# Attention in 64-token halves with their own decay reference, and TensorE's order written out: one change to a fused attention and expert kernel

## The chip, the core and the metric

The kernel runs on one core of a Trainium2 chip. The core has five engines that run side by side, each with its own queue of instructions, and they wait for one another by semaphores. TensorE multiplies matrices into PSUM. VectorE (DVE in the profile) and ScalarE (ACT) work on SBUF and PSUM. GpSimd (POOL) works on SBUF. SyncE (SP) only issues transfers here, and ScalarE and GpSimd issue some too. The metric is the device time of one execution in microseconds (us). A time is the median of several executions; the profile comes from one execution of its own.

## What is computed

Two parts, one after the other. The attention is a gated linear recurrence over 768 tokens, for 4 batches of 8 heads with 48 columns each. The experts are a balanced assignment of 3072 tokens to 8 experts of 384 tokens each, and a two-layer network per expert.

```
f = 1 / (1 + exp(-f_logit))
for t in range(S):
    state = f[t][:, None] * state + outer(k[t], v[t])     # 48 x 48 per head
    y[t] = q[t] @ state
x = y with the heads side by side                         # 3072 x 384
logits = x @ w_gate                                       # 3072 x 8
order = argsort(-logits.flatten())                        # tokens go to experts, best first,
                                                          # 384 tokens at most for each
out[tokens of e] = relu(x[tokens of e] @ w1[e]) @ w2[e]
```

## The kernel before

**Attention.** The recurrence is worked in chunks of 128 tokens, 24 of them (6 of one batch, c = 0 to 5, for 4 batches, and the four batches take turns). With g = -log f, the sum L of g from a reference token to token t turns the decay into factors: q is multiplied by exp(-L) and k by exp(L). In before the reference lies in the middle of the chunk of 128. Inside a chunk, the products of all q and k (`scores`, tile A) are masked to the lower triangle with a predicated copy (tile am) and multiplied by v (`outputs`, tile Y). What came from earlier chunks sits in a state of 48 by 48 for each head. It is moved to the chunk's reference by a factor gl (tile R, made by GpSimd) and multiplied by q into the same Y. The state is R plus the chunk's own sum of k times v (`states`, tile dS).

**Stages and steps.** `attention(first, last)` is a software pipeline. In step s, stage n works on chunk s - n. The stages of before are `decays` (f to g), `gates` (L, the factors eq and ek, the sums "ends" over each half of the chunk, gl, and qg and kg), `states` (the transposes T of qg and kg, R and dS), `scores`, `outputs`, `transposed` (x transposed for the next stage, tile X) and `gate` (the router's logits, and x with its logits written to DRAM as xd). Loads of f, q, k and v are issued by SP two chunks ahead in the program, and run as far ahead as buffers allow: five for f, q and k, eight for v. The order of the instructions on each engine is set by a scheduler, except where `tc.manual_schedule` names an engine: there it stays as the program has it. Each engine then takes its instructions strictly in that order.

**PSUM.** PSUM has eight banks. Six rotate among the tiles L, T, A, dS and X, and two hold Y. A tile that takes a bank waits until the readers of the tile six places earlier are done.

**Shapes.** A matmul's stationary operand fills 128 rows and up to 128 columns of the array, or a part: the profile writes 128*64 where it has 64 columns and 48*64 where it has 48 rows. Matmuls on different parts of the array run at the same time. The profile shows two records for each float32 matmul, and one for a transpose.

**Routing and experts.** After the attention come the router's search (a chain of small DVE and TensorE instructions) and the experts' networks (lines 495 and 506). The latter are written in a fixed order in which pieces of network are placed between the search's instructions. GpSimd gathers rows of xd for each expert (`fetch`, tile xe) and the logits of 768 leftover tokens (tile lg). `load_weights` loads 3.1 MB for each expert in two transfers. The first two experts' weights have memory of their own (pool `early`), the next three take the attention's memory when it is free. In before, expert 0's weights load during the attention. Of expert 1, w1 waits until the rows of expert 0 have been fetched (`behind`: ScalarE copies one fetched number into the tile, and the transfer has to follow that copy). Its w2 and the next experts' weights have no such wait.

Of the kernel before, what the change touches and what calls it, by code (L numbers as in the profile page):

```python
# [10 lines left out]
FP32 = mybir.dt.float32  # L11
# [13 lines left out]
def kernel(  # L25
# [49 lines left out]
    spans = const([128, NT, 2, HP], FP32, "spans")  # L75
# [6 lines left out]
    def kept(shape, dtype, name):  # L82
# [5 lines left out]
    mask = kept([128, 128], I32, "mask")  # L88
    nc.vector.tensor_copy(out=mask[:], in_=wcum[:])
    nc.vector.tensor_scalar(out=wcum[0:64, :], in0=wcum[0:64, :],  # L90
                            scalar1=-1.0, scalar2=None, op0=ALU.add)


    ind = kept([128, 2], FP32, "ind")
    nc.vector.memset(ind[:], 0.0)
    nc.vector.memset(ind[0:64, 0:1], 1.0)
    nc.vector.memset(ind[64:128, 1:2], 1.0)
# [6 lines left out]
    a_bufs = [kept([128, 2, HP, 128], FP32, f"am{i}") for i in range(NB)]  # L104
# [29 lines left out]
    def gates(G):  # L134
        i = G["i"] % NB
        g = g_bufs[i]
        L = ps("L")
        Lv = L[:, 0:D].rearrange("t (h d) -> t h d", d=DH)
        nc.tensor.matmul(out=Lv, lhsT=wcum[:], rhs=g[:, :, 0:DH], start=True, stop=True)  # L139
        ends = L[:, D:D + 2 * HP].rearrange("p (n a) -> p n a", a=HP)  # L140
        for hp in range(HP):
            for r in range(2):
                nc.tensor.matmul(out=ends[DP * r:DP * r + DP, :, hp], lhsT=g[:, 2 * hp + r, :],  # L143
                                 rhs=ind[:], start=True, stop=True)
        eq = work.tile([128, H, DH], FP32, name="eq", tag="eq")
        ek = work.tile([128, H, DH], FP32, name="ek", tag="ek")
        dl = work.tile([128, H, DH], FP32, name="dl", tag="dl")
        nc.vector.tensor_scalar(out=dl[:], in0=Lv, scalar1=LIMIT, scalar2=-LIMIT,  # L148
                                op0=ALU.min, op1=ALU.max)
        nc.scalar.activation(out=eq[:], in_=dl[:], func=AF.Exp, bias=0.0, scale=-1.0)  # L150
        nc.scalar.activation(out=ek[:], in_=dl[:], func=AF.Exp, bias=0.0, scale=1.0)  # L151
        span = spans[:, G["i"]]
        nc.vector.tensor_copy(out=span, in_=ends)

        if G["c"]:
            gl = work.tile([128, HP], FP32, name="gl", tag="gl", bufs=3)
            nc.gpsimd.tensor_tensor(out=gl[:], in0=span[:, 0], in1=spans[:, G["i"] - B, 1],  # L157
                                    op=ALU.add)
            nc.scalar.activation(out=gl[:], in_=gl[:], func=AF.Exp, bias=0.0, scale=-1.0)
            G["gl"] = gl  # L160
        qg, kg = q_bufs[i], k_bufs[i]
        nc.vector.tensor_tensor(out=qg[:, :, 0:DH], in0=G["q"][:], in1=eq[:], op=ALU.mult)  # L162
        nc.gpsimd.tensor_tensor(out=kg[:, :, 0:DH], in0=G["k"][:], in1=ek[:], op=ALU.mult)  # L163
        G.update(qg=qg, kg=kg)

    def states(G):
        b, c, v_ = G["b"], G["c"], G["v"]
        for nm, t, copy in (("qT", G["qg"], nc.scalar.copy), ("kT", G["kg"], nc.vector.tensor_copy)):
# [8 lines left out]

        R = None
        if c:
            R = work.tile([128, HP, DH], FP32, name="R", tag="R", bufs=5)  # L180
            nc.gpsimd.tensor_tensor(
                out=R[:], in0=state[b][:],
                in1=G["gl"][:].unsqueeze(2).to_broadcast((128, HP, DH)), op=ALU.mult)
        G["R"] = R
        if c == NCH - 1:
            return
        dS = ps("dS")
        for hp in range(HP):
            for r in range(2):
# [1188 lines left out]
```

## Time and profile before

| | us |
|---|---|
| median of 9 runs | 488.05 |
| lowest and highest run | 486.75 and 496.04 |
| the profiled execution's own time | 489.63 |
| its span, from first to last instruction | 487.8 |
| attention: last logits copied at | 170.7 |
| TensorE busy between 30 and 140 | 108.5 of 110 |
| TensorE busy between 168 and 190 (search) | 13.0 of 22 |
| TensorE busy between 222 and 488 (experts) | 254.1 of 266 |
| transfers' busy share between 30 and 140 | 0.89 |

A line of a group view names the source line, the engine, the operation, the tiles (out<-in), the shapes and the count. In a timeline, the first two numbers are the start and the length from the first start to the last end of the records that are merged in the line. In brackets is how long the engine had been idle and what ended that. "PEld" are weight loads of TensorE. A wait's line ends with its total, how many there were and the longest. Times of start are counted from the span's start.

### The profile page before, as it was taken

What the parts mean: (1) busy time and instruction counts of PE and PEld (TensorE: products, weight loads), DVE (VectorE), ACT (ScalarE), POOL (GpSimd) and SP (SyncE); (2) the same over time, 40 slices, a digit from 0 to 9 for tenths busy, and PEclk for the clock granted to TensorE, in tenths of its full rate; (3) what the DMA queues carried; (4) which work ended last, traced back from release to release, by engine and by line L of the source; (5) the groups of instructions that cost most, each with busy time, mean ns of one, the idle gap of its engine ahead of it and who ended that gap; (6) DMA issues with size and microseconds to landing.
All of it is one profiled execution on the core that took longest, in us unless ns stands there. A gap on an engine that the chain in (4) does not pass through costs nothing.

```text
span 487.8 us, 11676 instructions
## 1 busy us (share of the span) xinstructions
PE 454.0 (93%) x4996; PEld 322.4 (66%) x4996; DVE 157.6 (32%) x507; ACT 138.4 (28%) x366; POOL 105.5 (22%) x157
## 2 busy tenths in 40 slices
PE   2999999999999948999999999899999999999991
PEld 1678887887788735756566665768887656556550
DVE  7366556556566765023333332400000000000000
ACT  3355555545344200212121211213332221212200
POOL 3123343433133104710000100320003301301010
PEclk9999999999999959999999999999999999999997
DMA  9986989889941178970000000225993200200000
GB/s 153 187 165 147 187 178 189 187 187 260 251 159 38 69 262 307 265 272 17 6 28 1 32 1 16 55 63 176 315 321 93 71 0 34 66 16 34 0 34 20
DMA packets 118542, 59.28 MB, mean 122 GB/s; under 512 B 101841, under 2 KB 113105, under 8 KB 118481
## 3 DMA queue, kind: packets, MB, share of 16 engines
q1 hardware_dynamic: 111760, 44.06, 36.4%
q0 software_dynamic: 3264, 9.56, 6.5%
q10 hardware_dynamic: 3456, 4.82, 2.8%
q8 instruction: 41, 0.67, 0.6%
q14 instruction: 21, 0.16, 0.1%
HBM read 48.89 MB, written 9.54 MB: 120 GB/s over the span
## 4 chain that ended last, share of the span: by engine, by line
PE 71%; issue 16%; DVE 5%; POOL 5%; DMA 2%; ACT 0%; POOLq 0%; DVEq 0%
PE O L506 20%; PE H L495 19%; PE Y L225 5%; PE T L171 4%; PE L L139 4%; PE A L208 4%; PE L L143 3%; PE Y L235 2%; PE dS L190 2%; PE X L249 2%; PE cnt L564 2%; DMA lg<-xd,at_l 2%; PE X L260 2%; PE Xe L484 1%; POOL out_dram L512 1%
## 5 line engine op out<-in xcount | busy, mean ns | idle before, releaser
L495 PE MATMUL H<-xeT,w 128*128 128x256 f32 (+2 forms) x624 | 135.2, 369 | 1.9 <-DVE beyond L783 1.4
L506 PE MATMUL O<-w,hT 128*128 128x384 f32 x384 | 136.6, 494 | 0.0
L495 PEld LDWEIGHTS H<-xeT,w 128*128 128x128 f32 x624 | 97.7, 191 | 28.8 <-issue 1.6
L506 PEld LDWEIGHTS O<-w,hT 128*128 128x128 f32 x384 | 68.8, 190 | 37.0 <-issue 0.4
L512 POOL DMA_INDIRECT out_dram<-o,tok x24 | 23.5, 980 | 222.5 <-ACT o L511 218.3
L499 ACT ACTIVATE hT<-H 128x256 f32<-128x256 f32 (+2 forms) x104 | 38.3, 368 | 98.1 <-PE H L495 96.8
L213 DVE COPY_PREDICATED am<-mask,A 128x512 f32<-128x512 int32 x48 | 32.5, 730 | 31.1 <-PE A L208 31.1
L511 ACT COPY o<-O 128x384 f32<-128x384 f32 x24 | 11.5, 479 | 80.5 <-PE O L506 73.9
L545 POOL DMA_INDIRECT xe<-xd,tok x24 | 23.2, 966 | 42.3 <-DVE numb L299 28.9
L163 POOL TENSOR_TENSOR kg<-k,ek 128x384 f32<-128x384 f32 x24 | 25.5, 1062 | 27.8 <-ACT ek L151 22.0
L139 PE MATMUL L<-g,wcum 128*128 128x384 f32 x48 | 23.8, 580 | 7.4 <-DVE linef L333 7.4
L208 PE MATMUL A<-qT,kT 48*64 48x128 f32 x768 | 27.1, 278 | 0.8 <-issue 0.8
L225 PE MATMUL Y<-v,am 128*64 128x48 f32 x768 | 27.5, 224 | 0.0
L225 PEld LDWEIGHTS Y<-v,am 128*64 128x64 f32 x768 | 24.4, 138 | 3.9 <-issue 3.7
L487 ACT COPY xeT<-Xe 128x384 f32<-128x384 f32 x24 | 11.5, 478 | 43.4 <-PE Xe L484 43.4
L143 PEld LDWEIGHTS L<-ind,g 128*64 128x64 f32 x384 | 14.0, 145 | 14.7 <-issue 14.7
L208 PEld LDWEIGHTS A<-qT,kT 48*64 48x64 f32 x768 | 21.7, 137 | 1.3 <-issue 1.0
L564 PEld LDWEIGHTS <-above 128*31 128x31 f16 x264 | 8.8, 97 | 19.5 <-issue 10.5
L150 ACT ACTIVATE eq<-dl 128x384 f32<-128x384 f32 x24 | 12.6, 523 | 29.0 <-DVE dl L148 28.4
L148 DVE TENSOR_SCALAR dl<-L 128x384 f32<-128x384 f32 x24 | 13.4, 558 | 21.6 <-PE L L143 21.6
L171 PE MATMUL T<-ident,qg 128*128 128x128 f32 x96 | 16.6, 299 | 1.8 <-DVE qg L162 1.8
L157 POOL TENSOR_TENSOR gl<-spans 128x4 f32<-128x4 f32 x20 | 4.0, 201 | 64.4 <-DVE logits L265 44.7
(179 smaller groups left out, 459.7 us busy)
## 6 DMA issues: line engine op xcount, KB each, us to landing
w<-in_moe_w_dram SPq DMA_DIRECT2D x16, 1536.0 KB, 8.4
xd<-x ACTq DMA_DIRECT2D x24, 196.0 KB, 3.4
f<-in_f_logit_dram SPq DMA_DIRECT2D x24, 192.0 KB, 4.6
q<-in_q_dram SPq DMA_DIRECT2D x24, 192.0 KB, 4.7
k<-in_k_dram SPq DMA_DIRECT2D x24, 192.0 KB, 4.8
v<-in_v_dram SPq DMA_DIRECT2D x24, 192.0 KB, 4.6
xe<-xd,tok POOLq DMA_INDIRECT x24, 3.8
out_dram<-o,tok POOLq DMA_INDIRECT x24, 2.6
```

Of the source, the lines that this page charges most:

```text
L139: nc.tensor.matmul(out=Lv, lhsT=wcum[:], rhs=g[:, :, 0:DH], start=True, stop=True)
L143: nc.tensor.matmul(out=ends[DP * r:DP * r + DP, :, hp], lhsT=g[:, 2 * hp + r, :], rhs=ind[:], start=True, stop=True)
L163: nc.gpsimd.tensor_tensor(out=kg[:, :, 0:DH], in0=G["k"][:], in1=ek[:], op=ALU.mult)
L171: nc.tensor.transpose(out=T[:, 128 * hp:128 * hp + 128], in_=t[:, 2 * hp:2 * hp + 2, :].rearrange("t h d -> t (h d)"), identity=ident[:])
L208: nc.tensor.matmul(out=A[par][HC * j:HC * j + HC, 128 * hp:128 * hp + 128], lhsT=G["kT"][rows, hp, HC * j:HC * j + HC], rhs=G["qT"][rows, ...
L213: nc.vector.copy_predicated(am[:, par], mask[:].unsqueeze(1).to_broadcast((128, HP, 128)), A[par][:].rearrange("s (a t) -> s a t", t=128))
L225: nc.tensor.matmul(out=Y[par][HC * j:HC * j + HC, DH * hp:DH * hp + DH], lhsT=G["am"][:, par, hp, HC * j:HC * j + HC], rhs=G["v"][:, 2 * h ...
L495: nc.tensor.matmul(out=L["H"][:, 0:w], lhsT=slots[e][0][:, d, 128 * ft:128 * ft + 128], rhs=xT[:, d, 0:w], start=(d == 0), stop=(d == DC - 1))
L499: nc.scalar.activation(out=hT[:, ft, 0:w], in_=L["H"][:, 0:w], func=AF.Relu)
L506: nc.tensor.matmul(out=L["O"][:, 0:D], lhsT=hT[:, ft, 128 * i:128 * i + 128], rhs=slots[e][1][:, ft, :], start=(ft == 0), stop=(ft == FC - 1))
L512: nc.gpsimd.indirect_dma_start(out=outs[next(tiles)][:, :], out_offset=bass.IndirectOffsetOnAxis(ap=token(e, first_block + i), axis=0), in ...
L545: nc.gpsimd.indirect_dma_start(out=t[:], out_offset=None, in_=xd[:, :], in_offset=bass.IndirectOffsetOnAxis(ap=token(e, i), axis=0))
```

## The change

- **Halves.** The 128 tokens of a chunk become two halves of 64, each with a reference of its own in its middle. Matrix `wcum` becomes two blocks, the mask is 64 wide, and the sums over the chunk are taken for its four quarters. `scores` multiplies each half with itself alone: 64 columns instead of 128. What the second half owes to the first goes by the state: each chunk now has two R and two dS (except the last chunk of a batch, with one dS), and two updates of the state. Chunks with c = 0 get an R for their second half.
- **Y.** The products of am and v have 64 rows instead of 128. They are laid out so that upper and lower rows of the array write different banks. Some parts of a chunk's output then lie in two places. ScalarE copies one of them to SBUF (tile cross), and DVE adds them into x.
- **No clipping copy.** ScalarE's exponentials read L from PSUM. DVE's copy with limits (tile dl) is gone.
- **TensorE's order.** The attention's TensorE instructions stay as the program has them: L, transposes and X (128*128), then A, Y and dS (64 rows by 64 columns), then ends and the logits (128*64). Stages are split for that: `gates` into `cumulated` and `lengths`, `states` into `turned` and `states`. Ends and logits share a bank of their own (`step_bank`).
- **Small moves.** The logits go into x by GpSimd instead of ScalarE. Expert 1's weights load with expert 0's during the attention. The weights of experts 2, 3 and 4 now wait, w1 and w2 alike, for the fetched rows.

```diff
-    def gates(G):
+    def cumulated(G):
         i = G["i"] % NB
         L = ps("L")
...
-        nc.vector.tensor_scalar(out=dl[:], in0=Lv, scalar1=LIMIT, scalar2=-LIMIT,
-                                op0=ALU.min, op1=ALU.max)
-        nc.scalar.activation(out=eq[:], in_=dl[:], func=AF.Exp, bias=0.0, scale=-1.0)
-        nc.scalar.activation(out=ek[:], in_=dl[:], func=AF.Exp, bias=0.0, scale=1.0)
+        nc.scalar.activation(out=ek[:], in_=Lv, func=AF.Exp, bias=0.0, scale=1.0)
+        nc.scalar.activation(out=eq[:], in_=Lv, func=AF.Exp, bias=0.0, scale=-1.0)
+        qg, kg = q_bufs[i], k_bufs[i]
+        nc.gpsimd.tensor_tensor(out=kg[:, :, 0:DH], in0=G["k"][:], in1=ek[:], op=ALU.mult)
+        nc.vector.tensor_tensor(out=qg[:, :, 0:DH], in0=G["q"][:], in1=eq[:], op=ALU.mult)
...
+    def lengths(G):
+        r = step_bank()
+        ends = r[:, 0:4 * HP].rearrange("p (n a) -> p n a", a=HP)
...
+        nc.vector.tensor_copy(out=span, in_=ends)
+        gl = work.tile([128, 2, HP], FP32, name="gl", tag="gl", bufs=3)
+        nc.gpsimd.tensor_tensor(out=gl[:, 1], in0=span[:, 1], in1=span[:, 2], op=ALU.add)
+        first = 0 if G["c"] else 1
         if G["c"]:
+            nc.gpsimd.tensor_tensor(out=gl[:, 0], in0=span[:, 0], in1=spans[:, G["i"] - B, 3],
                                     op=ALU.add)
+        nc.scalar.activation(out=gl[:, first:2], in_=gl[:, first:2], func=AF.Exp, bias=0.0,
+                             scale=-1.0)
...
+    def states(G):
+        last = 1 if c == NCH - 1 else 2
+        for j in range(last):
+            dS = ps("dS")
+            half = slice(HC * j, HC * j + HC)
+            for hp in range(HP):
+                for r in range(2):
+                    nc.tensor.matmul(
+                        out=dS[DP * r:DP * r + DP, DH * hp:DH * hp + DH],
+                        lhsT=G["kg"][half, 2 * hp + r, :], rhs=v_[half, 2 * hp + r, :],
+                        start=True, stop=True)
...
+        for j in range(2):
+            if c or j:
+                R = work.tile([128, HP, DH], FP32, name="R", tag="R", bufs=8)
+                nc.gpsimd.tensor_tensor(
+                    out=R[:], in0=state[b][:],
+                    in1=G["gl"][:, j].unsqueeze(2).to_broadcast((128, HP, DH)), op=ALU.mult)
...
+                    nc.vector.tensor_tensor(out=state[b][:], in0=sums[j], in1=R[:], op=ALU.add)
...
     def scores(G):
+                        out=A[par][half, HC * hp:HC * hp + HC],
+                        lhsT=G["kT"][rows, hp, half],
+                        rhs=G["qT"][rows, hp, half], start=True, stop=True)
...
     def outputs(G):
+                        out=spot(j, par, j, hp, True), lhsT=G["am"][half, par, hp, :],
+                        rhs=G["v"][half, 2 * hp + par, :],
...
+                nc.scalar.copy(out=cross[HC:128, par], in_=Y[par][HC:128, W:2 * W])
+                nc.vector.tensor_tensor(
+                    out=xv[HC * j:HC * j + HC, par], in0=heads(Y[j][HC:128, 0:W]),
+                    in1=heads(cross[HC:128, par]), op=ALU.add)
...
     def gate(G, to=None):
-        nc.scalar.copy(out=G["x"][:, D:DX], in_=X[:, D:D + E])
+        nc.gpsimd.tensor_copy(out=G["x"][:, D:DX], in_=logits[:, G["b"] * NCH + G["c"]])
         row = S * G["b"] + C * G["c"]
         nc.scalar.dma_start(out=xd[row:row + C, :], in_=G["x"][:])
...
-    stages = (decays, gates, states, scores, outputs, transposed, gate)
+    stages = ((decays, 0), (cumulated, 1), (turned, 2), (transposed, 5), (scores, 3),
+              (outputs, 4), (states, 2), (lengths, 1), (gate, 6))
...
+    PE_ALONE = {mybir.EngineType.PE}
...
         if behind is not None:
             nc.scalar.copy(out=w1[0:1, 0, 0:1], in_=behind)
+            nc.scalar.copy(out=w2[0:1, 0, 0:1], in_=behind)
...
+    with tc.manual_schedule(engines=PE_ALONE):
+        attention(6, ALL - 4)
...
+        load_weights(0, early, 0)
+        load_weights(1, early, 1)
...
             for e in range(NA):
-                if e:
-                    load_weights(e, pools[e], e, rows[0, 1][0:1, 0:1] if e == 1 else None)
+                if e > 1:
+                    load_weights(e, pools[e], e, rows[0, 1][0:1, 0:1])
```

## The prediction

> **What bounds the kernel now.** I read the page's busy shares and its chain, then the busy time by windows, then TensorE alone through one step of the attention, then the other engines' rows, and last the waits on transfers.
>
> ```profile
> span 487.8 us, 11676 instructions
> PE 454.0 (93%) x4996; PEld 322.4 (66%) x4996; DVE 157.6 (32%) x507; ACT 138.4 (28%) x366; POOL 105.5 (22%) x157
> PE 71%; issue 16%; DVE 5%; POOL 5%; DMA 2%; ACT 0%; POOLq 0%; DVEq 0%
> ```
> TensorE is busy nearly everywhere and carries the chain, so its time saved in the attention (to about 171 us) moves the end, unless something else becomes late. One step, TensorE only (start, length to the last end, group, count of records):
> ```profile
> 97.30 0.67 PE L190 MATMUL dS<-v,kg 128*64 128x48 f32 x16
> 97.90 0.91 PE L139 MATMUL L<-g,wcum 128*128 128x384 f32 x2
> 98.74 0.63 PE L143 MATMUL L<-ind,g 128*64 128x2 f32 x16
> 99.23 0.50 PE L260 MATMUL X<-wg,xT 128*64 128x8 f32 x12
> 99.66 0.55 PE L249 MATMUL X<-ident,x 128*128 128x128 f32 x3
> 100.14 1.14 PE L225 MATMUL Y<-v,am 128*64 128x48 f32 x32
> 101.20 0.68 PE L235 MATMUL Y<-R,qT 48*64 48x48 f32 x32
> 101.71 1.07 PE L208 MATMUL A<-qT,kT 48*64 48x128 f32 x32
> 102.71 0.66 PE L171 MATMUL T<-ident,qg 128*128 128x128 f32 x4
> 103.20 0.60 PE L171 MATMUL T<-ident,kg 128*128 128x128 f32 x4
> 103.73 0.67 PE L190 MATMUL dS<-v,kg 128*64 128x48 f32 x16
> ```
> Start to start, a step is 103.73 - 97.30 = 6.43 us: dS 0.60, L 0.84, ends 0.49, gate 0.43, X 0.48, Y 1.06, YR (L235) 0.51, A 1.00, T 0.49 + 0.53. Per record, Y takes 33 ns and YR 16: both have 48 columns, but YR's matmuls alternate between the upper and lower 64 rows of the array. The other engines' prices come from these rows:
> ```profile
> 59.03 0.34 DVE L197 TENSOR_TENSOR st<-dS,R 128x192 f32<-128x192 f32 x1
> 61.00 0.20 POOL L157 TENSOR_TENSOR gl<-spans 128x4 f32<-128x4 f32 x1 [3.56 <-PE X L249]
> 61.52 0.55 DVE L162 TENSOR_TENSOR qg<-q,eq 128x384 f32<-128x384 f32 x1
> 61.66 0.19 ACT L159 ACTIVATE gl<-gl 128x4 f32<-128x4 f32 x1
> 61.93 0.34 ACTq L268 DMA_DIRECT2D xd<-x  x1
> 62.89 0.50 POOL L181 TENSOR_TENSOR R<-st,gl 128x192 f32<-128x192 f32 x1
> 63.63 1.35 DVE L213 COPY_PREDICATED am<-mask,A 128x512 f32<-128x512 int32 x2 [1.56 <-PE A L208]
> ```
> And the loads and the routing's gather, among the waits:
> ```profile
> POOL f L129 <- DMA f<-in_f_logit_dram: 13.3, 11, 3.3
> DVE lg L303 <- DMA lg<-xd,at_l: 12.2, 1, 12.2
> ```
>
> **TensorE's step after.** Gate precedes L, so L keeps 0.84. T and X follow in the same shape: eight T at 0.49 per four are 0.98, three X at that rate 0.37. A streams 64 columns instead of 128: between YR's 0.51 (its shape but for 16 columns) and its own 1.00; I take 0.51 plus 0.17, the gap that the weight loads show ahead of Y and of T where the shape changes. Y becomes 64 rows by 64 columns, rows alternating, so between 0.51 (YR) and 1.06 (its own); YR's pattern is the nearer, 0.51. YR stays 0.51. dS goes from 16 records to 32, eight matmuls on the upper rows and then eight on the lower: between 0.51 (if rows overlapped) and 1.06 (32 of Y's records, which share rows as these do); 1.06. Ends 0.49 plus one 0.17, gate 0.43. Sum 0.84 + 0.98 + 0.37 + 0.68 + 0.51 + 0.51 + 1.06 + 0.66 + 0.43 = 6.04. That counts some shape changes twice, as L's 0.84 and T's rate hold theirs. The lower end: L at 0.645 (a pair of 384-column records of O, 12 in 3.87 in the chain), T and X at 0.107 each (a sixth of that), A, Y, YR and dS 0.51, ends 0.49, gate 0.43, and three changes of 0.17 give 5.3. I take 5.8, nearer to the rows that include everything. TensorE saves 0.63 of 6.43.
>
> Here a rule speaks against the change. The row first: YR starts a record every 16 ns. The Trainium skill, "TensorE: Matmul & The Clock Gate", section "Back-to-back issue gap", holds that starts never come closer than about 25 ns however few columns stream. By it A, Y and YR would be 0.80 each, an estimate, and the step 6.9, slower than before. The trace has already gone below that floor with four 64x64 tiles in turn, so the measurement decides.
>
> **The other engines' loop.** The scheduler's new order makes a ring within each step that the old order lacks (there ScalarE issued the xd transfer after ek, and DVE waited for TensorE). Following queues and waits: ScalarE gl 0.24 with the hop (hops of 0.05, as gl to the xd rows show); POOL R of the first half 0.48 to the next start; POOL's new copy of the logits into x 0.25 (gl's row); ScalarE's xd issue 0.34; ek 0.43 to the next start; eq 0.57 with hop; DVE qg 0.47, xT 0.47; two predicated copies of 256 columns 0.73 (bounds 0.32, two 8-column copies of 0.16, and 1.35, the row; half the columns plus the fixed 0.16); the add that joins cross and Y 0.26; state add 0.39 with hop; POOL R of the second half 0.56 with hop; second state add 0.26; spans 0.21; two gl sums 0.37. Sum 6.03 us. In steps 12 to 15 and 18 to 21 the order is exactly this. In the other six of steps 8 to 21 either xT runs before qg (less 0.47) or spans before the second state add (about less 0.5): 5.55, below TensorE. Each new price has bounds of 0.16 (the smallest copy) and 0.55 (a 384-column pass), so the ring may be 5.5 to 6.9.
>
> The clip of L (0.56 on DVE, 24 times) goes, but costs no more than that: it lay beside TensorE's work. The cross copies, half-width x copies and the second R are new; off the ring they fit in ScalarE's 10.2 busy of 20 us and POOL's 7.3. If that cover failed, R's 0.5 a step would be 12 us over 24.
>
> **Steps summed.** Steps 8 to 21: eight at 6.03 and six at 5.8 against 6.43: 3.2 + 3.8 = 7.0. Steps 5 to 7 (the first chunks, half of YR new in them): TensorE 5.8 less 0.25 of YR, and in step 5 less 0.43 of gate, against 5.61, 5.97, 5.97: 0.5 + 0.4 + 0.4 = 1.3. Steps 22 to 24 (dS halved, where before had none): 5.27 against 5.63, together 1.1. Step 25: 0.4. The emptying pipeline: A and Y shorter by 0.5 each, twice Y, less 0.5 for the longer way from Y to x: 1.0. The start, where TensorE was slow until 23.7 (L 1.65 instead of 0.91) and its first L waited 7.4 for DVE: memsets of am halve from 0.91, but TensorE has more dS; 0, bounds -2 and +2. Together 10.8.
>
> **Transfers.** SP in-order loads took 5.16 us a chunk from 60.0 to 85.8 with no gap in its queue, so a pace of 5.8 still fits. Before, POOL's early clips of f, waiting on loads, cost TensorE about 2.5 us in all (steps of 6.73, 6.71 and 7.63). After, POOL clips three f's in a row in step 16, ahead of the second R, and f of chunk 22 can only be issued when its buffer frees then: about 3 us (landing 4.6 less what is idle), and 1 elsewhere. Net -1.5; bounds +2.5 (all waits gone) and -9.
>
> Expert 1's weights now load in the attention behind the last q, k, v on SP: nothing waits for them. Experts 2 to 4 load behind the first fetched rows, with six tiny ScalarE copies (0.19 each at most) ahead of the first xeT copy; TensorE waits later for lg in any case. The six lg gathers, 8.4 us for the last, keep their place behind POOL's issues of 0.95 and met full queues before too; 0, bounds +1 and -9.4 (if all three experts' 9.4 MB had to land first). The expert stage keeps its order.
>
> Net 10.8 - 1.5 = 9.3 saved. The profiled execution is 489.63 us (487.8 span and 1.8 around it), 1.6 above the median of 488.05. 489.63 - 9.3 = 480.3, and by the median 478.7.
>
> **Rivals.**
> - TensorE sets the pace and is quick. dS on half rows overlaps and the ring stays under 5.5: steps 8 to 21 at 5.4 give 14.4, with the 3.8 of the other steps and 2 for cheaper dS there, less 1.5: 469.3. For it: YR's 16 ns. Against: dS's order, eight matmuls on the same rows.
> - The saving is eaten: the ring at 6.4. Then 14 steps save nothing, the rest 3.8 less 1.5: 485.7. For it: ten hops between engines, each perhaps 0.04 longer. Against: hops of 0.04 to 0.08 in the rows.
> - Slower: late f loads enter the ring. POOL stands still for f while R, and through it spans, gl and ek, wait. Before, 11 waits averaged 1.2 us and lay mostly beside TensorE. If each of steps 5 to 21 took 1.2 on the path, 20.4 against 10.8 gives 497.6. It decides from 0.64 us per step (10.8 / 17). For it: the DMA share was already 0.83 to 0.99. Against: kg of chunk 13 now needs 17 clips before it instead of 18, so POOL asks for f a chunk later.
>
> **How the numbers follow.** Chances: forecast 0.50, quick TensorE 0.22, eaten 0.16, slower 0.12. The forecast's own range is 474 to 484. For 8 in 10 I go to 467 (the quick case with its start's bound) and 488 (the eaten case with 2 us of waits). Half a percent, 2.4 us, is about what this kernel's times can tell from no change. Faster by that: forecast 0.50, quick 0.22 and 0.07 of eaten, which ends at the border, 0.79; within it 0.08 of eaten; slower 0.12 and the last 0.01.
>
> **What the profile after would show.** Right: A near 0.5 to 0.7, Y near 0.5, dS near 1.0 in a step of 5.8 to 6.1; ScalarE's ek released late by the xd issue while TensorE shows gaps of 0.2 to 0.5 a step; logits done near 161. Wrong: A or Y at 25 ns a record or more; steps under 5.5; long waits of POOL for f; lg landing later than 9 us after its issue.

## The result, and the profile after

The changed kernel is slower: 515.4 us median of 10 runs (511.9 to 520.8) against 488.5 of 31 runs before, a ratio of 1.054 (95% interval 1.051 to 1.057). The forecast was 478.7, range 467 to 488. The profiled execution took 512.5 us; its page:

```profile
span 510.7 us, 12759 instructions
PE 447.4 (88%) x5444; PEld 324.7 (64%) x5444; DVE 168.6 (33%) x560; ACT 152.1 (30%) x395; POOL 127.0 (25%) x229
PE 58%; issue 16%; DVE 7%; POOL 7%; DMA 5%; ACT 3%; SPq 2%; ACTq 0%; POOLq 0%; DVEq 0%
```

TensorE works 6.6 us less than before (447.4 against 454.0, although part of it now runs at half clock) and carries 58% of the chain instead of 71%. The span grew by 22.9. Where, by the starts of the steps (taken at the copies of the logits, which stand at a step's start before and at its end after; for after's step 6, which has none ahead of it, at its L):

| stretch | before, us | after, us | change |
|---|---|---|---|
| start to step 6 | 36.0 | 30.3 | -5.7 |
| steps 6 to 23 | 115.6 | 131.6 | +15.9 |
| step 24 to the last logits (pipeline empties) | 19.1 | 28.8 | +9.7 |
| last logits to the end | 317.1 | 320.0 | +2.9 |

A middle step took 7.3 us on average instead of 6.42. Four of these steps in the windows view of after (window, its length, then each engine's busy time with its count of instructions, then the granted clock, the transfers' share and GB/s):

```profile
core 0: us, PE busy (x) PEld busy (x) DVE busy (x) ACT busy (x) POOL busy (x), PEclk, DMA share, GB/s
46.19:52.51 6.32, 5.41 (x170) 4.77 (x169) 4.51 (x12) 3.96 (x10) 3.25 (x8) 1.00 0.91 187
52.51:60.38 7.87, 6.88 (x170) 5.71 (x169) 4.07 (x12) 4.34 (x12) 2.99 (x8) 0.79 1.00 187
60.38:68.06 7.68, 5.75 (x170) 5.02 (x171) 4.62 (x11) 4.54 (x12) 3.77 (x8) 1.00 0.85 170
68.06:74.45 6.39, 5.35 (x170) 4.71 (x171) 4.30 (x11) 4.12 (x11) 2.98 (x7) 1.00 0.88 185
```

TensorE has 5.4 us of work in a step of full clock, less than the 5.8 forecast, and idles 0.9 to 1.9 us of each of the four. Before, it was busy 108.5 of 110 us. Three kinds of step stand out up to the last loads (38.8 to 149.8 us): six at full clock take 6.3 to 7.2 (mean 6.77); six in which the clock fell take 7.4 to 8.3 (mean 7.87); three with a pause of TensorE that no wait explains take 7.3 to 8.2 (mean 7.74). One undisturbed step of after in the timeline, the steps of its chain:

```profile
74.34 0.91 PE L142 MATMUL L<-g,wcum 128*128 128x384 f32 x2
...
76.54 1.09 DVE L149 TENSOR_TENSOR qg<-q,eq 128x384 f32<-128x384 f32 x1
...
77.35 0.65 PE L257 MATMUL Y<-R,qT 48*64 48x48 f32 x32
...
78.02 0.76 DVE L226 COPY_PREDICATED am<-mask,A 128x256 f32<-128x256 int32 x2
78.08 0.31 ACT L271 COPY cross<-Y 64x192 f32<-64x192 f32 x1 [0.66 <-PE Y L257]
78.67 0.64 PE L158 MATMUL G<-ind,g 128*64 128x4 f32 x16
78.81 0.36 DVE L272 TENSOR_TENSOR x<-Y,cross 64x192 f32<-64x192 f32 x1
79.20 0.36 DVE L211 TENSOR_TENSOR st<-dS,R 128x192 f32<-128x192 f32 x1
...
79.64 0.51 POOL L202 TENSOR_TENSOR R<-st,gl 128x192 f32<-128x192 f32 x1 [2.42 <-DVE st L211]
...
80.18 0.36 DVE L211 TENSOR_TENSOR st<-dS,R 128x192 f32<-128x192 f32 x1 [0.23 <-POOL R L202]
...
80.46 0.17 DVE L161 COPY spans<-G 128x16 f32<-128x16 f32 x1
...
80.68 0.52 PE L296 MATMUL G<-wg,xT 128*64 128x8 f32 x12 [1.38 <-DVE spans L161]
```

The last line is the one that the prediction lacks. The logits' matmuls (gate, L296) write the bank that holds the ends (L158), so they wait until DVE has copied the ends to spans. The ends were done by 79.3; DVE copies them at 80.46, because spans stands in its queue behind the two state adds, and these behind R and behind the add of cross, which needs Y from TensorE. In TensorE's fixed order L comes after gate. So TensorE can't run ahead: gate, its work from L to Y, then cross, x, state, R, state, spans and the next gate make one ring. The waits of the whole run:

```profile
POOL R L202 <- DVE st L211: 28.6, 12, 3.6
PE G L296 <- DVE spans L161: 18.5, 19, 2.3
POOL f L133 <- DMA f<-in_f_logit_dram: 9.0, 6, 3.2
PE G L158 <- issue: 5.4, 3, 2.3
```

TensorE waited for spans in 19 steps, 18.5 us in all.

### The profile page after: what moved, and what is told of

It is laid out like the page before. It is cut to its first block, busy times and chain, and to the rows that moved or that the text cites. A ratio compares the mean times of both kernels' runs of the same rounds, so it can differ in the third digit from the quotient of the medians.

```text
span 510.7 us, 12759 instructions
## 1 busy us (share of the span) xinstructions
PE 447.4 (88%) x5444; PEld 324.7 (64%) x5444; DVE 168.6 (33%) x560; ACT 152.1 (30%) x395; POOL 127.0 (25%) x229
## 4 chain that ended last, share of the span: by engine, by line
PE 58%; issue 16%; DVE 7%; POOL 7%; DMA 5%; ACT 3%; SPq 2%; ACTq 0%; POOLq 0%; DVEq 0%
PE O L555 20%; PE H L544 18%; PE T L176 4%; DMA f<-in_f_logit_dram 3%; PE L L142 3%; PE G L296 2%; PE cnt L613 2%; DMA lg<-xd,at_l 2%; PE A L221 2%; DVE st L211 2%; PE Y L257 1%; SPq L127 1%; PE X L285 1%; POOL R L202 1%; PE Xe L533 1%
## 5 line engine op out<-in xcount | busy, mean ns | idle before, releaser
L202 POOL TENSOR_TENSOR R<-st,gl 128x192 f32<-128x192 f32 x44 | 22.3, 507 | 62.3 <-DVE st L211 28.6
L296 PE MATMUL G<-wg,xT 128*64 128x8 f32 x288 | 13.9, 217 | 18.5 <-DVE spans L161 18.5
L148 POOL TENSOR_TENSOR kg<-k,ek 128x384 f32<-128x384 f32 x24 | 24.4, 1017 | 19.1 <-ACT ek L145 19.1
L181 DVE COPY kT<-T 128x512 f32<-128x512 f32 x24 | 16.6, 691 | 26.5 <-PE T L176 26.5
L296 PEld LDWEIGHTS G<-wg,xT 128*64 128x64 f32 x288 | 11.8, 154 | 20.7 <-DVE spans L161 20.2
L149 DVE TENSOR_TENSOR qg<-q,eq 128x384 f32<-128x384 f32 x24 | 22.7, 944 | 3.9 <-ACT eq L146 3.5
L271 ACT COPY cross<-Y 64x192 f32<-64x192 f32 x44 | 13.8, 314 | 33.6 <-PE Y L257 21.7
L192 PE MATMUL dS<-v,kg 64*64 64x48 f32 x704 | 22.2, 223 | 0.0
L158 PE MATMUL G<-ind,g 128*64 128x4 f32 x384 | 16.3, 204 | 5.4 <-issue 5.4
L176 PEld LDWEIGHTS T<-ident,kg 128*128 128x128 f32 x96 | 14.2, 164 | 10.8 <-issue 5.3
L192 PEld LDWEIGHTS dS<-v,kg 64*64 64x64 f32 x704 | 20.0, 137 | 0.3 <-issue 0.3
```

What stands on the lines that cost most here:

```text
L176: nc.tensor.transpose(out=T[:, 128 * hp:128 * hp + 128], in_=t[:, 2 * hp:2 * hp + 2, :].rearrange("t h d -> t (h d)"), identity=ident[:])
L192: nc.tensor.matmul(out=dS[DP * r:DP * r + DP, DH * hp:DH * hp + DH], lhsT=G["kg"][half, 2 * hp + r, :], rhs=v_[half, 2 * hp + r, :], start ...
L202: nc.gpsimd.tensor_tensor(out=R[:], in0=state[b][:], in1=G["gl"][:, j].unsqueeze(2).to_broadcast((128, HP, DH)), op=ALU.mult)
L296: nc.tensor.matmul(out=r[half, at:at + E], lhsT=G["xT"][:, d, half], rhs=wg[:, d, :], start=(d == 0), stop=(d == DC - 1))
```

## The experiments

They ran on several chips, on which before took between 488 and 498 us; each ratio is to before on the same chip. Steps can be compared across chips: before's step at full clock took 6.43 us in all three profiles of it that keep its TensorE work (before itself, without the clip, without the loads).

### Which wait makes the ring

**A bank for gate.**

```diff
-        r, at = (G["X"], D) if to is not None else (step_bank(), 64)
+        r, at = (G["X"], D) if to is not None else (ps("G2"), 0)
```

> The changed kernel with one edit: the logits' matmuls get a bank of their own, so they no longer share one with the ends and no longer wait for DVE's copy of spans. Theory A (this wait holds TensorE, and with it L and ek, inside the ring of the other engines): steps 8 to 21 fall from 7.25 us to about 6.3, the time from 515.4 to about 500. Theory B (two ways from spans to ek are about equally long, the one by gate and L, the other by gl, R, the copy of the logits and ScalarE's transfer issue; in the step at 60 us L ended at 61.18 and the issue at 61.52): ek keeps waiting for the issue, the step loses at most 0.3, the time is 510 to 515.

Ratio 1.021 (1.015 to 1.027) instead of 1.054, the largest gain of all single edits; times 488.5 that is 499 us, as theory A had it. The steps between the first and the nineteenth logits fall from 7.23 to 6.59 us on average, not quite to 6.3. Theory B falls: the way by ScalarE's transfer issue does not take over.

**The transfer of x one step later.**

```diff
+    def written(G):
         row = S * G["b"] + C * G["c"]
         nc.scalar.dma_start(out=xd[row:row + C, :], in_=G["x"][:])
...
+    stages = ((decays, 0), (cumulated, 1), (written, 7), (turned, 2), ...
```

> The changed kernel with one edit: x and its logits are written to DRAM one step later (x has six buffers), so ScalarE's transfer issue ahead of ek finds its logits long copied and waits for nothing. Theory A: no change, 513 to 517. Theory B: ek now waits for L alone, which ended 0.3 us before the issue did; at most 0.3 per step, 510 to 515. Only if GpSimd's way by R and the copy of the logits alone sets the ring do some 0.5 us a step go, to about 506.

Ratio 1.054 (1.046 to 1.063): no gain that this interval shows, though the steps of the profiled execution took 7.04 us on average instead of 7.23. The issue ahead of ek, a link of the ring that the prediction had summed, does not set the time. GpSimd's copy of the logits stayed where it was; that the ring closes without it is read from the step shown further down.

**eq before ek**, so that DVE's qg no longer runs beside GpSimd's kg (two lines swapped, and the two products after them).

> The changed kernel with one edit: ScalarE makes eq before ek, so DVE's qg starts before GpSimd's kg instead of beside it. If qg's 1.1 us (0.55 alone) beside kg is a term of the ring, as both theories have it, the step loses 0.4 to 0.7 us: 504 to 508. If the ring does not pass through qg: 513 to 517.

Ratio 1.044 (1.037 to 1.051), steps 7.24 on average in the profiled execution. At most one per cent; the interval touches that of the changed kernel, so even this is not certain. Mean qg between 30 and 165 us falls from 0.92 to 0.76 us. The average step hides something: of the first fifteen steps, the five at full clock took 6.2 to 6.5 us (mean 6.40, against 6.77 in after), but the clock fell in the other ten, against six in after. So qg beside kg may well cost some 0.4 us of an undisturbed step; the time of the whole does not show it.

**Lengths before scores.**

```diff
-    stages = ((decays, 0), (cumulated, 1), (turned, 2), (transposed, 5), (scores, 3),
-              (outputs, 4), (states, 2), (lengths, 1), (gate, 6))
+    stages = ((decays, 0), (cumulated, 1), (turned, 2), (transposed, 5), (lengths, 1),
+              (scores, 3), (outputs, 4), (states, 2), (gate, 6))
```

> The changed kernel with one edit: stage lengths (ends, spans, the gl sums) stands before scores instead of at the end of the step, so spans, gl and R no longer wait for the state adds in DVE's order. Both theories: the ring is cut, since neither gate nor R waits for the end of DVE's step; the step falls by 1 us or more, to what TensorE needs (about 5.3) or at most 6.2, the time to 488 to 500. If the step is long for other reasons (late f, DVE and GpSimd in each other's way): 508 or more.

Ratio 1.039 (1.033 to 1.046), steps 6.59. Spans no longer stand behind the state adds, and the steps shorten by as much as with a bank for gate: another cut through the same ring. By the ratio that is 508 us, where 488 to 500 was expected. Part of the difference lies ahead of the steps: in the profiled execution the first logits came at 43.8 us, 6.0 later than with the bank, as the clock fell again during the start.

### What the loads cost

**The ring without loads**, and the same two for comparison, with a bank for gate and for before:

```diff
+            old = G["i"] - (8 if nm == "v" else 5)
+            if old >= 0:
+                G[nm] = chunks[old][nm]
+                continue
```

> The kernel with a bank for gate, which leaves out the loads of f, q and k from the sixth chunk on and of v from the ninth (the old tiles are used again, so the output is not the attention's). It had steps between 5.2 and 8.7 us, pauses of TensorE of 0.7 to 2.5 us that no wait explains, and GpSimd waiting for f. Theory C (transfers make both: late f, and pauses because what TensorE needs for issuing arrives by the same transfer engines): pauses and waits for f vanish, every step is 5.3 to 5.6, the attention ends some 15 us earlier. Rival D (pauses and long steps come from the engines themselves: the ring, qg beside kg, the clock): steps keep their mean of 6.59 within 0.3.

> The changed kernel, leaving out the loads of f, q and k from the sixth chunk on and of v from the ninth (old tiles are used again, the output is not the attention's). With a bank for gate and without these loads the steps took 5.66 us on average. If gate's wait on spans holds TensorE in the ring: 6.2 to 6.5 a step here, from 7.30, pauses of TensorE gone; the loads then cost the changed kernel some 0.9 a step and the ring alone is as long as before's step. If the wait only matters when something is late: 5.6 to 5.8.

> The kernel before, leaving out the same loads (the output is not the attention's). TensorE was busy 108.5 of 110 us, so steps stay at 6.42, or 6.3 without the three steps that waited for f (6.73, 6.71 and 7.63): the time falls by 2 us at most. If transfers slowed it in another way (TensorE's operands, instructions): steps of 6.0 to 6.2.

The changed kernel without its later loads is no faster: ratio 1.054 (1.036 to 1.071), and 7.24 us a step. Its pauses are gone (none over 0.4 us from 43 to 170 us), and no f is loaded that could be late, yet the ring stands: of its first fifteen steps, the seven at full clock took 6.50 to 6.84 us (mean 6.67, against 6.77 with the loads). That the average came out the same is in part chance, since the clock fell in the other eight (mean 8.06), against six with the loads. One of the seven in the timeline:

```profile
71.38 0.65 PE L261 MATMUL Y<-R,qT 48*64 48x48 f32 x32
...
72.17 0.32 ACT L275 COPY cross<-Y 64x192 f32<-64x192 f32 x1 [1.38 <-PE Y L261]
72.56 0.36 DVE L276 TENSOR_TENSOR x<-Y,cross 64x192 f32<-64x192 f32 x1
...
72.95 0.36 DVE L215 TENSOR_TENSOR st<-dS,R 128x192 f32<-128x192 f32 x1
...
73.39 0.51 POOL L206 TENSOR_TENSOR R<-st,gl 128x192 f32<-128x192 f32 x1 [2.42 <-DVE st L215]
73.93 0.36 DVE L215 TENSOR_TENSOR st<-dS,R 128x192 f32<-128x192 f32 x1 [0.23 <-POOL R L206]
74.20 0.17 DVE L165 COPY spans<-G 128x16 f32<-128x16 f32 x1
...
74.42 0.52 PE L300 MATMUL G<-wg,xT 128*64 128x8 f32 x12 [1.08 <-DVE spans L165]
```

This step began with its gate at 67.92, 6.50 earlier. In order: gate 0.45; L, T, X, A and Y to the end of YR, 3.48 (L starts at 68.37, YR's successor at 71.85); to cross 0.32; to x 0.39; to the first state add 0.39; to R 0.44; to the second add 0.54; to spans 0.27; to gate 0.22. The sum is 6.50, and 3.93 of it is TensorE's.

With a bank for gate the steps at full clock come down to what TensorE needs, and TensorE has no gap. Two of them, in the windows view, both without the later loads:

```profile
60.95:66.26 5.31, 5.31 (x170) 4.69 (x169) 4.28 (x12) 3.63 (x11) 2.91 (x8) 1.00 0.11 41
66.26:71.51 5.25, 5.25 (x170) 4.72 (x169) 4.29 (x14) 3.73 (x11) 2.93 (x8) 1.00 0.12 41
```

And two steps without the bank, again without the later loads, the second with the clock fallen:

```profile
68.49:74.99 6.50, 5.42 (x170) 4.77 (x171) 4.45 (x11) 3.69 (x11) 3.03 (x8) 1.00 0.11 36
88.29:97.56 9.27, 8.23 (x170) 7.02 (x171) 4.21 (x11) 3.46 (x11) 2.93 (x7) 0.68 0.08 25
```

So the shared bank alone lengthens an undisturbed step by 1.2 us, from 5.3 to 6.5. With the bank apart the loads do matter: 5.66 a step without them and 6.68 with them, both from the third logits to the nineteenth. In the latter run TensorE paused 13.4 us in all between 38 and 156 us, ten times for 0.4 to 2.4 us each; without the loads four pauses of 0.3 to 0.8 us are left there. One pause of the run with the loads in its timeline (the idle time is in the brackets):

```profile
101.28 0.52 PE L158 MATMUL G<-ind,g 128*64 128x4 f32 x12 [2.41 <-issue]
```

Theory C holds there and only there. The pauses seem to go with the transfers of instructions. The instruction queue (q8) moves a packet of 16 KB every 5.0 us in that run; over the whole run its 45 packets, 0.74 MB, are 68 bytes for each of TensorE's 10,888 records, so it probably feeds TensorE. Each of the eight pauses over 0.6 us ended 1.2 to 1.7 us after such a packet's end (the one shown at 101.28, its packet from 98.42 to 99.61), and each of the three in after 1.4 us after one. That TensorE stood waiting for its next instructions, held up by the loads, fits this; no run changed the instruction transfers alone, so it is not shown.

Before without its later loads kept steps of 6.43 us, without the long ones, and had its last logits at 167.9 instead of 170.7: the loads cost it under 3 us. (After the attention this run goes through far more work, 5,066.9 us in all, and only its attention is read. The run with a bank and without loads took 491.9 us, beside 488.5 of before.)

### The order

**TensorE left to the scheduler**, and the old order of the stages:

```diff
-    with tc.manual_schedule(engines=PE_ALONE):
+    with ExitStack():
```

> The changed kernel with TensorE's order left to the scheduler throughout the attention (the logits' matmuls then stand after the first transposes of the step, and the last steps are interleaved anew); everything else as changed. If the fixed order costs the emptying pipeline its 9 us (the last four logits came over 9.98 us, before over 8.0, and the step from 172 to 190 had TensorE waiting for x), logits 20 to 23 follow in 8 us or less and some 8 to 10 us of the 22.9 come back there. If gate ahead of L is the other half, the steps fall by about 0.6 as in the run with a bank for gate, and the ratio to before goes from 1.054 to about 1.01. If the order is not to blame, the ratio stays above 1.04.

```diff
-    stages = ((decays, 0), (cumulated, 1), (turned, 2), (transposed, 5), (scores, 3),
-              (outputs, 4), (states, 2), (lengths, 1), (gate, 6))
+    stages = ((gate, 6), (transposed, 5), (outputs, 4), (scores, 3), (turned, 2), (states, 2),
+              (cumulated, 1), (lengths, 1), (decays, 0))
```

> The changed kernel with the stages in the order of before (gate first, decays last; the logits in x's bank again), and TensorE left to the scheduler: dS, L, ends, gate, X, Y, A, T, the order of before, with the halves' matmuls. Theory G (the grouped order, in which the logits, the spans and L stand at the seam of two steps, closes the ring): steps of 5.5 to 5.9 as TensorE's work needs, ratio 0.97 to 0.99. Theory H (the halves themselves cost: two state updates in series, late f, TensorE's pauses and the clock that falls after them, whatever the order): steps of 6.3 to 6.8 as with a bank for gate, ratio 1.01 to 1.03.

Ratios 1.044 (1.040 to 1.048) and 1.052 (1.043 to 1.060). In the first run the scheduler's order cut the ring by itself: steps at full clock without a pause took 5.6 to 6.0 us, about what the prediction had for TensorE (5.8). The ratio hardly moved, because the clock fell: in the profiled execution, the longest of the four, it stood at half from 67 to 107 us, with TensorE busy without a gap. A step at full clock, and the four steps of that stretch:

```profile
113.90:119.53 5.63, 5.60 (x170) 4.79 (x171) 4.53 (x11) 3.99 (x12) 3.10 (x8) 1.00 0.61 133
67.36:106.88 39.52, 39.52 (x677) 33.51 (x678) 17.61 (x45) 15.94 (x42) 12.41 (x30) 0.50 0.68 138
```

In the four runs the mean granted clock was 0.90 to 0.93, where before on the same chip had 0.97 to 0.98. The emptying pipeline, for which this edit was made, hardly gained: 27.0 us from the eighteenth to the last logits instead of 28.8, where some 8 to 10 was hoped for.

In the second run, the old order, theory G falls: with gate out of the shared bank, the halves are as slow as in the new order. Four of its steps in the windows view:

```profile
43.23:49.39 6.16, 6.08 (x154) 4.94 (x155) 4.18 (x12) 3.54 (x9) 3.21 (x8) 1.00 0.78 151
58.43:68.61 10.18, 10.18 (x170) 8.21 (x171) 4.30 (x12) 4.41 (x12) 2.31 (x9) 0.50 0.94 185
68.61:78.78 10.17, 10.17 (x170) 8.20 (x171) 4.21 (x12) 3.76 (x11) 3.17 (x8) 0.50 0.71 131
127.09:133.65 6.56, 6.32 (x170) 5.04 (x171) 4.19 (x12) 3.64 (x10) 3.22 (x8) 1.00 0.64 133
```

There are two reasons. At full clock TensorE itself is busy 6.1 us in the first of them, which has 154 records, and 6.3 us in the last, with all 170, where the new order needs 5.4: in the old order nearly all that the halves save on TensorE is lost again (before's step took 6.43). And the clock fell to half, where a step's records took 10.2 us with TensorE busy without a gap, in three of eighteen steps entirely and in seven more in part.

**Three edits together**: the bank, lengths before scores, and TensorE free in the last four steps.

> The changed kernel with three edits: a bank for gate, lengths before scores, and TensorE's order left to the scheduler from the router's bounds on (the last four steps). If each removes its own part (the bank 0.64 a step, lengths what is left of the ring, the free end 8 us), the ratio to before goes from 1.054 to 0.99 to 1.005. If the bank and lengths remove the same wait (each gave 0.64 a step) the steps stay at 6.5 and the ratio is about 1.01. If the free end gives nothing: 1.02.

Ratio 1.034 (1.028 to 1.040), worse than the bank alone. The parts do not add.

### The clock

**Idle matmuls** on TensorE (128x128 by 384 columns, 16 bits). `e12_warm` and `e11_bank_warm` have three ahead of the ends in each step, and more in the last ones; `e19_warm_wait` puts the three behind the ends, where TensorE waits; `e20_bank_warmtail` has only those of the last steps.

```diff
+    def busy(to, n):
+        for _ in range(n):
+            nc.tensor.matmul(out=to[:, 0:384], lhsT=warm[:, 0:128], rhs=warm[:], start=True, stop=True)
...
+        busy(r, 3)                  # ahead of the ends
...
+        if G.get("i", 0) >= 20:
+            busy(X, 5)              # ahead of x's transposes
...
+        busy(r, 6)                  # in the bounds
```

> The changed kernel with idle matmuls added on TensorE: three of 128x128 by 384 columns in 16 bits ahead of the ends in each step, five ahead of x's transposes for the last four chunks, six in the router's bounds; they write a bank that is overwritten, and change no result. Theory E (TensorE's clock falls to half because the smaller matmuls and the gaps leave its array too idle, and the half clock lengthens the ring and the last steps): the granted clock in the attention goes from 0.83 to 0.91 back to 1.00, the last four logits follow in some 7 us instead of 9.98, the ratio to before goes from 1.054 to about 1.02. Rival F (the clock's falls are only a consequence; the ring and the pauses set the time): TensorE gets 0.5 us more per step in the ring, the ratio is 1.05 to 1.07.

> The same idle matmuls in the kernel with a bank for gate (ratio 1.021). Theory E: steps 6 to 23 fall from 6.59 to about 6.0, the last steps by 3 to 5 us; ratio 0.99 to 1.00. Rival F: nothing gained, TensorE has 0.5 us more work per step; ratio 1.02 to 1.04.

> The changed kernel with the idle matmuls in the place where TensorE waits: three behind the ends and ahead of gate in each step (into x's bank, long read), five ahead of x's transposes of the last four chunks, six in the bounds. Theory E (the clock lengthens the ring's steps): the steady steps keep full clock and take 6.5 to 6.8 us instead of 7.23 on average, 8 to 13 us in all, and the last steps lose 2 to 4: ratio 1.02 to 1.03 instead of 1.054. Rival F (the clock follows, and half clock costs the ring little): ratio 1.045 to 1.06.

> The kernel with a bank for gate (ratio 1.021), with idle matmuls only in the last steps: five ahead of x's transposes of the last four chunks, six in the bounds. The last four logits took 9.98 us at half clock there and 7.87 with these matmuls in the run that had them in all steps. If that is the clock alone, 2 to 4 us come off: ratio 1.012 to 1.017. If the last steps are a chain of the other engines: 1.02.

Ratios 1.073 (1.064 to 1.081), 1.057 (1.049 to 1.065), 1.051 (1.043 to 1.059) and 1.026 (1.019 to 1.033). Ahead of the ends they cost time, as they lie on the ring (with the bank, TensorE itself is the limit). In the place of the wait they cost nothing, and gain nothing: steps of 7.20 instead of 7.23, and the clock still fell (0.91 from 60 to 140 us, 0.94 without them). So theory E was not confirmed for the middle steps; idle matmuls of this size do not keep the clock up there, and what the clock costs there could not be taken away to be measured. That it costs is seen in the steps themselves (9.27 us against 6.50 above). In the last steps they do hold the clock. First the run with the bank and no idle matmuls, in the windows view:

```profile
160.00:170.00 10.00, 5.52 (x124) 4.61 (x120) 6.16 (x28) 1.90 (x7) 0.83 (x3) 0.57 0.10 34
170.00:180.00 10.00, 5.90 (x106) 4.96 (x106) 4.01 (x18) 1.55 (x5) 0.60 (x3) 0.50 0.16 59
```

Then the run with the bank and idle matmuls in the last steps:

```profile
160.00:170.00 10.00, 8.38 (x234) 6.88 (x227) 7.49 (x28) 3.08 (x10) 2.09 (x7) 1.00 0.13 44
170.00:180.00 10.00, 7.77 (x216) 5.70 (x214) 4.85 (x18) 2.50 (x8) 0.38 (x2) 1.00 0.12 43
```

There the stretch from the eighteenth to the last logits fell from 27.1 to 23.9 us. The whole run was none the faster for it (1.026 against 1.021, intervals overlapping); where the 3.2 us went was not followed up.

### Parts alone

**Before without the clipping copy.**

```diff
-        nc.vector.tensor_scalar(out=dl[:], in0=Lv, scalar1=LIMIT, scalar2=-LIMIT,
-                                op0=ALU.min, op1=ALU.max)
-        nc.scalar.activation(out=eq[:], in_=dl[:], func=AF.Exp, bias=0.0, scale=-1.0)
+        nc.scalar.activation(out=eq[:], in_=Lv, func=AF.Exp, bias=0.0, scale=-1.0)
```

> The kernel before with one part of the change alone: ScalarE's exponentials read L from PSUM and the copy with limits (tile dl) is left out, so the limits are no part of what it computes. The prediction put this part at nothing, as the 0.56 us on DVE lay beside TensorE's work: ratio 0.997 to 1.003. If the copy was in the way (DVE's queue): up to 24 times 0.2, ratio 0.99.

Ratio 1.0005 (0.996 to 1.005): nothing, as expected.

**Before with the masked columns of A left out.**

```diff
-                        out=A[par][HC * j:HC * j + HC, 128 * hp:128 * hp + 128],
+                        out=A[par][HC * j:HC * j + HC, 128 * hp + HC * j:128 * hp + 128],
```

> The kernel before with one narrow part of the change: where the mask leaves nothing, scores computes nothing (the second half's keys against the second half's queries alone, 64 columns instead of 128; DVE's predicated copy in four pieces instead of two). Chunks, references and order stay as before. TensorE was busy without gaps there, so what A loses comes off the end: 16 of 32 records at some 16 instead of 33 ns, 0.25 us a step over some 20 steps, 5 us: ratio 0.99, if TensorE stays the bound and its clock at 1.00. If the clock falls or late f takes it back: 0.997 to 1.01.

Ratio 1.023 (1.017 to 1.029), a miss. A gained nothing and DVE lost; two rows of its timeline:

```profile
100.12 2.44 DVE L215 COPY_PREDICATED am<-mask,A 64x512 f32<-64x512 int32 x4 [1.26 <-PE A L208]
...
105.59 1.06 PE L208 MATMUL A<-qT,kT 48*64 48x128 f32 x32
```

Half of A's records have half the columns, and the 32 take the same 1.0 us, as if the quarters of the array with 128 columns, beside which the others run, set the time alone. DVE's masked copy went from 1.35 to 2.44 us, and the first two steps from 5.97 to 7.07.

**The changed kernel with the weights loaded as before** (expert 1's back behind the fetched rows, no wait for the next ones).

> The changed kernel with the weights loaded as before (expert 1's w1 behind the fetched rows, its w2 and the next experts' weights without a wait). From lg's arrival to the end the changed kernel took 283.0 us against 281.4 before, and from the last logits to lg 37.0 against 35.7. If the new places of the loads make these 2.9, the ratio to before falls from 1.054 to about 1.048. If they are not to blame: 1.05 to 1.057.

Ratio 1.052 (1.045 to 1.060): no difference that these intervals can tell. The profile tells one. From the last logits to the end this run took 317.1 us, as before did (317.1), where after took 320.0; lg landed 35.6 us behind the last logits, as before, where after had 36.9. On the three chips where both kinds were profiled, that stretch was 317.0 to 317.4 us with the weights loaded as before, and 318.8 to 320.4 with the changed loads.

## Why the prediction was wrong

- **TensorE's step: right.** Forecast 5.8 between 5.3 and 6.04, measured 5.25 to 5.42. A, Y and YR took 0.51, 0.46 and 0.46, 14 to 16 ns a record; dS took 0.85 instead of 1.06. The measured pitch decided against the 25 ns that the prediction cites, as it had said.
- **"The other engines' loop": this step failed.** It assumed that TensorE runs ahead of the ring. The diff shows `step_bank()` shared by ends and logits, and the prediction's list of waits never asked who must have read that bank before gate may write it. The ring that resulted is another one than the one summed: 3.93 us of TensorE and 2.57 us from cross to the next gate, with neither qg nor ek nor the xd issue in the step that was added up. Its length, 6.5 in the run without loads and 6.77 on average in the undisturbed steps of after, is near the 6.4 of the rival "eaten", reached by other terms. Moving the xd issue gained nothing in the time, a bank for gate gave back 3.3 points of 5.4. In the fifteen steps to 149.8 us the profile has 22 us more than the forecast's mean of 5.93 a step: 12.6 are the ring (6.77 in every step), 6.6 the clock and 2.9 the pauses.
- **The clock falls: not priced at all.** Before, the granted clock was 1.00 from 30 to 170 us, after 0.91 (before first):

```profile
30.00:170.00 140.00, 137.73 (x3231) 112.21 (x3229) 88.57 (x215) 65.79 (x190) 45.14 (x80) 1.00 0.72 168
30.00:170.00 140.00, 115.84 (x3150) 100.41 (x3148) 85.31 (x212) 71.08 (x191) 59.58 (x136) 0.91 0.74 174
```

  After, six of the fifteen steps to 149.8 us had parts at half clock and took 1.1 us longer on average, as TensorE is on the ring. Where the scheduler's order had cut the ring, the ratio was still 1.044, with the clock at half for five whole steps of the profiled execution. TensorE's idle time is not the whole cause: there and in the old order the clock stayed at half while TensorE was busy without a gap.
- **One price in the ring was wrong as well.** qg was put at its 0.47, and took 1.09 beside kg. In the step shown it delays the masked copy, and this the add of cross. The Trainium skill, "SBUF — State Buffer", section "SBUF: two separate sides", says that VectorE with two SBUF inputs and GpSimd share a port pair, and that whichever starts second waits for the other's whole instruction. The trace agrees: 0.55 where qg starts first, as in every step of before; where kg was already running, 0.59 to 1.31, and qg then ended 0.41 us after kg did. The prediction took the 0.55 of a row in which qg ran first. Its 0.73 for the two masked copies is 0.76 by its own rule ((1.35 - 0.16) / 2 + 0.16), and they took 0.76.
- **"Steps summed": the emptying pipeline.** For the stretch from step 24 the forecast has about 1.8 saved (0.4 of step 24, 0.4 of step 25 and 1.0), measured are 9.7 lost. The longer way from Y to x was put at 0.5 in all; in the step after the bounds it takes 2.62 us, from 180.03 to 182.65, where before took 0.54 (two copies, the first line). Then the timeline of after:

```profile
164.28 0.54 ACT L241 COPY x<-Y 128x192 f32<-128x192 f32 x2 [1.26 <-PE Y L235]
...
180.03 0.31 ACT L271 COPY cross<-Y 64x192 f32<-64x192 f32 x1 [5.59 <-PE Y L257]
180.71 0.17 DVE L301 COPY logits<-G 128x8 f32<-128x8 f32 x1 [1.43 <-PE G L296]
180.91 0.36 DVE L272 TENSOR_TENSOR x<-Y,cross 64x192 f32<-64x192 f32 x1
...
181.16 0.34 ACTq L304 DMA_DIRECT2D xd<-x  x1
181.60 0.31 ACT L271 COPY cross<-Y 64x192 f32<-64x192 f32 x1 [1.26 <-DVE x L272]
181.94 0.71 ACT L279 COPY x<-Y 64x192 f32<-64x192 f32 x2
181.94 0.36 DVE L272 TENSOR_TENSOR x<-Y,cross 64x192 f32<-64x192 f32 x1 [0.68 <-ACT cross L271]
```

  The first add stands in DVE's queue behind the copy of the logits; the second cross waits for that add, with ScalarE's issue of xd between, and the second add for that cross. Half clock adds to it (0.50 from 180 to 195 us); the idle matmuls measured that part at 3.2 us in the run with the bank.
- **The start: not decided by this profile.** It gained 5.7 where 0 within 2 was said, because the full clock came earlier: L takes 0.91 instead of 1.65 from 15.85 us on, before only from 28.29. When it comes varies between executions whose starts are nearly the same: in the changed kernel without its later loads L still took 1.65 at 26.07, and step 6 began at 38.2, later than before; in before without the clip L took 0.91 from 19.09, and step 6 began at 31.6. How much of the 5.7 is the change's is open.
- **Transfers: net -1.5 forecast.** Without its later loads the changed kernel took the same time: the pauses went, and the clock fell in more steps. The slower rival had the right sign and the wrong mechanism: late f is not what made the time (six waits of GpSimd for f, 9.0 us, where before had eleven and 13.3).
- **Nothing for the clip:** borne out to half a per cent.
- **Nothing for the weights, bounds +1 and -9.4:** inside the bounds, but not nothing. The 2.9 us lost after the last logits go with the new places of the weights' loads: the run that puts only these back has 317.1 there again. Some 1.3 of them are there when lg lands; which transfer holds lg up is open.

Still open are what makes the clock fall in the middle steps, and whether TensorE's pauses are waits for instructions. No version of the changed kernel that computes the attention was faster than before.

## What to carry to other kernels

Before pricing a ring, list for every matmul who must have read its PSUM bank before it may write there: two small results in one bank tie the second's engine to the first's reader, and in a fixed order everything behind it. An engine that is saturated hides long chains of the others, and taking work from it pays only until the next chain is reached, which here lay at the old step's length. Look at the pipeline's end by itself: where nothing runs beside it, each added hop from one engine to another can count in full.

## What the runs showed of the hardware

- TensorE stayed at half clock while busy without a gap: 20.35 of 20.35 us from 58.43 to 78.78 in the run with the old order, 39.52 of 39.52 from 67.36 to 106.88 in the run with the scheduler's order. The Trainium skill, "TensorE: Matmul & The Clock Gate", part "The HAM clock gate", has full clock come back after one busy window of about 3.4 us. By what the trace calls busy, these runs disagree; the measurement decides.
- Three idle matmuls a step, 0.66 us in the timeline, did not keep the clock in the middle steps; 26 in the last steps did.
- Halving the columns of half of A's 32 records, which lie on other quarters of the array than the rest, left A at 1.0 us.
- TensorE pauses that no semaphore explains, three of 1.4 to 2.3 us in after and ten of 0.4 to 2.4 with a bank for gate, shrink to 0.8 us at most when the loads are left out. Those over 0.6 us in these runs end 1.2 to 1.7 us after a 16 KB packet of the instruction queue.
